# A decode attention kernel on one Trainium2 core: keys moving past stationary queries, softmax along the free axis, exponentials turned in 32x32 squares by VectorE

## The chip, the cores and the metric

The kernel runs on one core of one Trainium2 chip. The metric is the device time of one execution in microseconds. Three runs of the kernel before gave 127.4, 127.41 and 128.99 us, median 127.41 us. One further execution was profiled: it took 127.15 us, of which the profile's span (first to last instruction) is 125.4 us, at a mean granted TensorE clock of 0.97.

## What is computed

One decode step for a batch of B = 8 tokens: a layer norm, grouped-query attention over the last 1024 of 4096 cached keys, and a gated feed-forward part whose result multiplies the attention's. All inputs are bfloat16.

```python
# x: [8, 1, 512]; k_cache, v_cache: [8, 8, 4096, 128]; wq: [512, 4096]; wo: [4096, 512]
# w_gate, w_up: [512, 1792]; w_down: [1792, 512]
xn = layernorm(A_x)
W  = 1024                                             # window: the last W keys
q  = (xn @ wq) as [8, 32 heads, 1, 128]
k  = repeat(k_cache[:, :, 4096 - W:, :], 4, axis=1)   # 8 key heads, each for 4 query heads
v  = repeat(v_cache[:, :, 4096 - W:, :], 4, axis=1)
p  = softmax(einsum("bhqd,bhkd->bhqk", q, k) * 128 ** -0.5)
s  = einsum("bhqk,bhkd->bhqd", p, v) as [8, 1, 4096] @ wo
g  = silu((gelu(xn @ w_gate) * (xn @ w_up)) @ w_down)
out = A_x + s * g
```

The names B_x and A_x are two inputs; the kernel, like the reference, feeds the normalised A_x to both parts.

## The kernel before

Keys and values are read in 16 **quads** (`NQ`). A quad is one key head and four batch rows (`QG` = 4), 1024 keys each: 1 MB of keys and 1 MB of values. `load_set` brings one such megabyte in one DMA, issued by SP, into one of 16 ring buffers `ring_sb` of 128 partitions by 8 KB. Each partition holds 32 consecutive keys of one batch row. The DRAM side of that copy is written `"g (e c) d -> e g (c d)"`: the outer count is e (32 blocks of 32 keys), the next is g (the 4 batch rows), the inner run is 32 keys by 128 values, 8 KB. So the rows of the tile go 4 to a block: partition 4e + g.

SP issues all loads of the kernel in one fixed order: the feed-forward weights (w_gate, w_up, w_down), wq, the first two key quads (`LAG` = 2), then for every quad the keys of the quad two ahead and its own values, and after every second quad half a megabyte of wo. A tile of the ring is taken again once the work on its old content has ended. At most some eight loads are on their way at a time.

The order of the compute is written out by hand. After the feed-forward part and the query projection (with dummy matmuls, `keep_busy`, between them) the main loop runs over q = 0 to 17 and, in each, over four **steps** i. A step does on TensorE: eight transposes of 128x128 key squares into PSUM (`transposes`), eight score matmuls (`scores`) in which the transposed keys are stationary and 16 query columns move, and eight value matmuls for the quad two before (`values`). The transposed keys go from PSUM to SBUF in two parts, 640 columns by VectorE (`kTa`) and 384 by ScalarE (`kTb`).

Scores come out with keys on partitions and, in the free axis, 32 key columns by 16 query columns (4 batch rows by 4 heads), so three quarters of what is computed is between the key of one batch row and the query of another. A matmul per quad (`row_of`, `other`, L382) first puts -1e30 into those places. The maximum over keys is taken along the free axis by VectorE (`max_keys`, L404) and across partitions with a TensorE transpose and another reduction (`max_all`, L412, L414). Two small VectorE operations (L419, L422) lay its negative out on a diagonal, and a 512-column matmul (L433) adds it to the scores in PSUM. ScalarE takes the exponentials (L442). They already have keys on partitions, as `values` needs. `sums` adds them over partitions with eight matmuls by ones (L447) and inverts the sums. `normalise` scales the attention output and `project` multiplies it by wo.

Of the kernel before, what the change touches and what calls it, by code (L numbers as in the profile page):

```python
# [8 lines left out]
ACT = mybir.ActivationFunctionType  # L9
ALU = mybir.AluOpType  # L10
AX = mybir.AxisListType
BF16 = mybir.dt.bfloat16
FP32 = mybir.dt.float32
PSUM = bass.MemoryType.PSUM
# [3 lines left out]
def kernel(  # L18
# [28 lines left out]

    nc = tc.nc
    ctx.enter_context(tc.manual_schedule())

    B, Sq, D = A_x.shape
    Hkv, Sk, Dh = A_k_cache.shape[1], A_k_cache.shape[2], A_k_cache.shape[3]
    Hq = A_wq.shape[1] // Dh
    rep = Hq // Hkv
    W = min(4096, max(256, Sk // 4))
# [10 lines left out]
    QG = 4  # L66
    NB = QG
    NCS = QG * NSC
    VC = 4
    AC = 3  # L70
# [4 lines left out]
    QC = QG * rep  # L75
    SH = B // QG
# [8 lines left out]
    p_pool = ctx.enter_context(tc.tile_pool(name="p_pool", bufs=4))  # L85
# [4 lines left out]
    ps_mx = ctx.enter_context(tc.tile_pool(name="ps_mx", bufs=1, space=PSUM))  # L90
    ps_sum = ctx.enter_context(tc.tile_pool(name="ps_sum", bufs=1, space=PSUM))
# [5 lines left out]
    qT_all = persist.tile([P, B, Hq], BF16, name="qT_all")  # L97
# [12 lines left out]
    def load_set(cache, q):  # L110
        hkv, b = divmod(q * QG, B)
        t = buffer(NL)
        nc.sync.dma_start(
            out=t,
            in_=cache[b : b + QG, hkv, win0:Sk, :].rearrange(
                "g (e c) d -> e g (c d)", c=NCS
            ),
        )
        return t
# [48 lines left out]
    for q in range(NQ):  # L168
# [23 lines left out]
    nc.vector.memset(ones_pp, 1.0)  # L192

    row_of = consts.tile([QG, P // QG, QG], BF16, name="row_of")
    nc.vector.memset(row_of, 0.0)
    nc.gpsimd.affine_select(
        out=row_of,
        in_=row_of,
# [3 lines left out]
        pattern=[[0, P // QG], [1, QG]],  # L202
        channel_multiplier=-1,
    )
    other = consts.tile([QG, QG, rep], BF16, name="other")
    nc.vector.memset(other, MASK)
    nc.gpsimd.affine_select(
        out=other,
        in_=other,
        compare_op=ALU.not_equal,  # L210
        fill=0.0,
        base=0,
        pattern=[[1, QG], [0, rep]],
        channel_multiplier=-1,
    )

    LO = 32
    diag = []
    for i in range(2):
        t = consts.tile([LO + QC, QC], BF16, name=f"diag{i}")  # L220
        nc.vector.memset(t, 0.0)
        diag.append(t)
# [131 lines left out]
    nc.vector.tensor_copy(out=qT_all, in_=qT_ps.rearrange("p h b -> p b h"))  # L354


    kT, sc, pT, mxs, shift, recip = {}, {}, {}, {}, {}, {}

    def transposes(g):
        q, i = divmod(g, NB)  # L360
        kT_ps = ps_kT.tile([P, W], BF16, name="kT_ps")
        for c in range(NSC):
            n = i * NSC + c
            nc.tensor.transpose(  # L364
                kT_ps[:, c * P : (c + 1) * P],
                k_sb[q][:, n * Dh : (n + 1) * Dh],
                ident,
            )
        own = (NSC - AC) * P
        ta = kT_pool.tile([P, own], BF16, name="kTa")  # L370
        nc.vector.tensor_copy(out=ta, in_=kT_ps[:, 0:own])  # L371
        tb = kT_pool.tile([P, W - own], BF16, name="kTb")
        nc.scalar.copy(out=tb, in_=kT_ps[:, own:])  # L373
        kT[g] = [ta[:, c * P : (c + 1) * P] for c in range(NSC - AC)]
        kT[g] += [tb[:, c * P : (c + 1) * P] for c in range(AC)]

    def scores(g):
        q, i = divmod(g, NB)
        hkv, b = divmod(q * QG, B)
        if i == 0:  # L380
            sc[q] = ps_sc.tile([P, NCS, QC], FP32, name="sc_ps")
            nc.tensor.matmul(  # L382
                sc[q],
                row_of.rearrange("g e s -> g (e s)"),
                other.rearrange("g s j -> g (s j)")
                .unsqueeze(1)
                .to_broadcast([QG, NCS, QC]),
                start=True,
                stop=False,
                skip_group_check=True,  # L390
            )
        for c in range(NSC):
            nc.tensor.matmul(  # L393
                sc[q][:, i * NSC + c, :],
                kT[g][c],
                qT_all[:, b : b + QG, hkv * rep : (hkv + 1) * rep],
                start=False,
                stop=False,
                skip_group_check=True,
            )  # L400

    def max_keys(q):
        mx = small.tile([P, QC], FP32, name="mx")
        nc.vector.tensor_reduce(  # L404
            out=mx, in_=sc[q].rearrange("p c n -> p n c"), axis=AX.X, op=ALU.max
        )
        mxs[q] = mx

    def max_all(q):

        mxT_ps = ps_mx.tile([QC, P], FP32, name="mxT_ps")
        nc.tensor.transpose(mxT_ps, mxs[q], ident_f)  # L412
        nm = small.tile([QC, 1], FP32, name="nm")
        nc.vector.tensor_reduce(  # L414
            out=nm, in_=mxT_ps, axis=AX.X, op=ALU.max, negate=True
        )
        eye = ident_f[0:QC, 0:QC]
        parts = diag[q % 2]
        nc.vector.tensor_scalar(  # L419
            out=parts[0:QC, :], in0=eye, scalar1=nm[:, 0:1], scalar2=None, op0=ALU.mult  # L420
        )
        nc.vector.scalar_tensor_tensor(  # L422
            out=parts[LO : LO + QC, :],
            in0=eye,
            scalar=nm[:, 0:1],
            in1=parts[0:QC, :],
            op0=ALU.mult,
            op1=ALU.subtract,
        )
        shift[q] = parts  # L430

    def exponentials(q):
        nc.tensor.matmul(  # L433
            sc[q],
            ones_pp[0 : LO + QC, :],
            shift[q].unsqueeze(1).to_broadcast([LO + QC, NCS, QC]),
            start=False,
            stop=True,
            skip_group_check=True,
        )  # L440
        pT[q] = p_pool.tile([P, NCS, QC], BF16, name="pT")
        nc.scalar.activation(out=pT[q], in_=sc[q], func=ACT.Exp, scale=inv_sqrt_dh)  # L442

    def sums(q):
        sums_ps = ps_sum.tile([P, NB, QC], FP32, name="sums_ps")
        for c in range(NSC):
            nc.tensor.matmul(  # L447
                sums_ps,
                ones_pp,
                pT[q][:, c * NB : (c + 1) * NB, :],  # L450
                start=(c == 0),
                stop=(c == NSC - 1),
            )
        recip[q] = small.tile([P, QC], FP32, name="recip")
        nc.vector.tensor_reduce(  # L455
            out=recip[q],
            in_=sums_ps.rearrange("p c n -> p n c"),
            axis=AX.X,
            op=ALU.add,
        )  # L460
        nc.vector.reciprocal(out=recip[q], in_=recip[q])

    o_ps = {}

    def values(g):
        q, i = divmod(g, NB)
        if i == 0:
            o_ps[q] = ps_o.tile([P, VC, QC], FP32, name="o_ps")
        for c in range(NSC):
            n = i * NSC + c  # L470
            wide = VC if n + VC <= NCS else 1
            nc.tensor.matmul(  # L472
                o_ps[q][:, 0:wide, :],
                v_sb[q][:, n * Dh : (n + 1) * Dh],
                pT[q][:, n : n + wide, :],
                start=(n == 0),
                stop=(n == NCS - 1),
                skip_group_check=True,
            )

    def normalise(q):
        hkv, b = divmod(q * QG, B)
        nc.vector.tensor_tensor(  # L483
            out=oT_all[:, hkv * rep : (hkv + 1) * rep, b : b + QG].rearrange(
                "p j g -> p g j"
            ),
            in0=o_ps[q][:, 0, :].rearrange("p (g j) -> p g j", g=QG),
            in1=recip[q].rearrange("p (g j) -> p g j", g=QG),
            op=ALU.mult,
        )  # L490
# [18 lines left out]
    for q in range(NQ + LAG):  # L509
        v = q - LAG  # L510
        for i in range(NB):
            g = q * NB + i
            if g + 1 < NG:
                transposes(g + 1)
            if i == 1 and 1 <= q <= NQ:
                max_all(q - 1)
            if g < NG:
                scores(g)
            if v >= 0:
                if i == 0:  # L520
                    sums(v)
                values(v * NB + i)
            if i == 2 and 1 <= q <= NQ:
                exponentials(q - 1)
            if v >= SH and v % SH == 0 and i >= NB // 2:
                for h in range(2):
                    project((v // SH - 1) * rep + (i - NB // 2) * 2 + h)
        if v >= 0:
            normalise(v)
        if q < NQ:  # L530
            max_keys(q)
# [6 lines left out]
    sg_ps = ps_mx.tile([B, D], BF16, name="sg_ps", tag="mxT_ps")  # L538
# [35 lines left out]
```

## Time and profile before

| what | value |
|---|---|
| median of three runs | 127.41 us |
| the profiled execution, its own time | 127.15 us |
| its span | 125.4 us |
| TensorE matmul busy | 109.9 us (88%) |
| TensorE weight load busy | 85.5 us (68%) |
| VectorE busy | 64.3 us (51%) |
| ScalarE busy | 42.3 us (34%) |
| read from HBM over the span | 47.46 MB |

The table is read so: a busy TensorE is not TensorE at its peak, since matmuls are pipelined and their modelled durations overlap (a lone 128x128 transpose shows 0.22 us, eight in a row show 0.61 us from first start to last end). Busy shares are averages over the whole span; what limits a stage is seen in that stage's waits.

### The profile page before, as it was taken

The page shows a single profiled execution, that of the slowest core. Times are in us where ns is not written, and L with a number is a line of the kernel's source. Part 1 is how long each engine was busy: PE and PEld are TensorE (multiplying, and loading weights), DVE is VectorE, ACT ScalarE, POOL GpSimd, SP SyncE. Part 2 cuts the span into 40 slices and gives each one's busy share as a digit, 9 for nine tenths or more (in the row PEclk, how much of TensorE's full clock was granted, in tenths as well). Part 3 has the DMA queues.
Part 4 walks back from the last instruction along what each step waited for, and adds up shares of the span by engine and source line. Part 5 has one row for each costly group of instructions (what it writes and reads, how often), then busy time and mean ns, then how long its engine had stood idle before and what let it go on. Part 6 is the DMA issues. An engine that isn't in the chain of part 4 may idle for free.

```text
span 125.4 us, 4892 instructions
## 1 busy us (share of the span) xinstructions
PE 109.9 (88%) x2202; PEld 85.5 (68%) x2202; DVE 64.3 (51%) x200; ACT 42.3 (34%) x86; POOL 1.2 (1%) x7
## 2 busy tenths in 40 slices
PE   5997819897999999999997997969999998999780
PEld 1444315574777888878886876849888886788570
DVE  5200300101467767856866664744676675766531
ACT  4000500000356355453453434342536435344210
POOL 3000000000000000000000000000000000000000
PEclk9999995999999999999999999985999999999999
DMA  3999999999999999999999999999999999999600
GB/s 78 407 418 389 350 405 421 423 421 418 421 415 423 396 421 421 408 415 428 413 404 422 431 406 415 418 431 402 420 422 423 398 425 418 414 398 420 244 32 3
DMA packets 12373, 47.78 MB, mean 381 GB/s; under 512 B 816, under 2 KB 6720, under 8 KB 7744
## 3 DMA queue, kind: packets, MB, share of 16 engines
q1 hardware_dynamic: 12336, 47.46, 93.9%
q8 instruction: 17, 0.28, 0.9%
q14 instruction: 4, 0.03, 0.1%
q10 hardware_dynamic: 16, 0.01, 0.0%
HBM read 47.46 MB, written 0.01 MB: 378 GB/s over the span
## 4 chain that ended last, share of the span: by engine, by line
DMA 44%; PE 32%; SPq 9%; DVE 7%; ACT 4%; issue 2%; ACTq 0%
DMA ring_sb<-in_A_k_cache_dram 30%; DMA ring_sb<-in_A_v_cache_dram 14%; PE kT_ps L364 12%; PE o_ps L472 6%; PE sc_ps L393 6%; SPq L129 4%; DVE kTa L371 4%; ACT kTb L373 4%; SPq L143 3%; PE sc_ps L433 2%; PE sc_ps L382 2%; PE sT_ps L498 2%; PE sums_ps L447 2%; SPq L136 2%; DVE mx L404 1%
## 5 line engine op out<-in xcount | busy, mean ns | idle before, releaser
L373 ACT COPY kTb<-kT_ps 128x384 bf16<-128x384 bf16 x64 | 30.6, 479 | 55.7 <-DVE kTa L371 55.6
L371 DVE COPY kTa<-kT_ps 128x640 bf16<-128x640 bf16 x64 | 31.2, 489 | 23.3 <-PE kT_ps L364 22.7
L364 PE MATMUL kT_ps<-ident,ring_sb 128*128 128x128 bf16 x512 | 39.7, 221 | 3.0 <-DMA ring_sb<-in_A_k_cache_dram 3.0
L364 PEld LDWEIGHTS <-ring_sb 128*128 128x128 bf16 x512 | 29.7, 98 | 5.7 <-DMA ring_sb<-in_A_k_cache_dram 4.6
L472 PE MATMUL o_ps<-pT,ring_sb 128*128 128x64 bf16 (+1 forms) x512 | 24.7, 191 | 0.9 <-issue 0.7
L472 PEld LDWEIGHTS <-ring_sb 128*128 128x128 bf16 x512 | 19.1, 98 | 1.5 <-issue 0.8
L231 PE MATMUL idle_ps<-ones_w 128*128 128x512 bf16 x58 | 17.4, 434 | 1.5 <-DVE ones_w L177 1.5
L393 PEld LDWEIGHTS <-kTa 128*128 128x128 bf16 x320 | 14.8, 97 | 4.4 <-issue 2.0
L393 PE MATMUL sc_ps<-qT_all,kTa 128*128 128x16 bf16 x320 | 17.7, 171 | 0.0
L393 PE MATMUL sc_ps<-qT_all,kTb 128*128 128x16 bf16 x192 | 14.5, 171 | 1.3 <-ACT kTb L373 0.4
L393 PEld LDWEIGHTS <-kTb 128*128 128x128 bf16 x192 | 9.3, 96 | 2.9 <-ACT kTb L373 1.0
L404 DVE TENSOR_REDUCE mx<-sc_ps 128x16 f32<-128x512 f32 x16 | 10.9, 680 | 0.0
L442 ACT ACTIVATE pT<-sc_ps 128x512 bf16<-128x512 f32 x16 | 9.6, 602 | 2.4 <-PE sc_ps L433 2.4
L231 PEld LDWEIGHTS <-ones_w 128*128 128x128 bf16 x58 | 5.0, 102 | 6.3 <-issue 1.7
L433 PE MATMUL sc_ps<-diag,ones_pp 48*128 48x512 bf16 x16 | 6.2, 386 | 0.4 <-DVE diag L422 0.4
L447 PE MATMUL sums_ps<-pT,ones_pp 128*128 128x64 bf16 x128 | 6.5, 195 | 0.0
L382 PE MATMUL sc_ps<-other,row_of 4*128 4x512 bf16 x16 | 6.4, 398 | 0.0
L309 PEld LDWEIGHTS <-ring_sb 128*128 128x128 bf16 x56 | 2.3, 107 | 5.4 <-DMA ring_sb<-in_B_w_down_dram 3.8
L498 PEld LDWEIGHTS <-wo_sb 128*128 128x128 bf16 x128 | 4.3, 96 | 2.4 <-issue 2.4
L455 DVE TENSOR_REDUCE recip<-sums_ps 128x16 f32<-128x64 f32 x16 | 3.6, 224 | 4.3 <-PE sums_ps L447 4.3
L498 PE MATMUL sT_ps<-oT_all,wo_sb 128*128 128x8 bf16 x128 | 5.4, 167 | 0.3 <-DVE oT_all L483 0.3
L309 PE MATMUL fT_ps<-hT_sb,ring_sb 128*128 128x8 bf16 x56 | 2.3, 170 | 3.3 <-DMA ring_sb<-in_B_w_down_dram 3.3
(54 smaller groups left out, 58.7 us busy)
## 6 DMA issues: line engine op xcount, KB each, us to landing
ring_sb<-in_A_k_cache_dram SPq DMA_DIRECT2D x16, 1024.0 KB, 18.7
ring_sb<-in_A_v_cache_dram SPq DMA_DIRECT2D x16, 1024.0 KB, 18.6
ring_sb<-in_A_wq_dram SPq DMA_DIRECT2D x4, 1024.0 KB, 14.3
wo_sb<-in_A_wo_dram SPq DMA_DIRECT2D x8, 512.0 KB, 17.5
ring_sb<-in_B_w_gate_dram SPq DMA_DIRECT2D x2, 896.0 KB, 4.7
ring_sb<-in_B_w_up_dram SPq DMA_DIRECT2D x2, 896.0 KB, 8.1
ring_sb<-in_B_w_down_dram SPq DMA_DIRECT2D x2, 896.0 KB, 14.1
x_sb<-in_A_x_dram ACTq DMA_DIRECT2D x1, 8.0 KB
```

What stands on the lines that cost most here:

```text
L231: nc.tensor.matmul(idle_ps, ones_w[:, 0:P], ones_w, start=True, stop=True)
L364: nc.tensor.transpose(kT_ps[:, c * P : (c + 1) * P], k_sb[q][:, n * Dh : (n + 1) * Dh], ident,)
L371: nc.vector.tensor_copy(out=ta, in_=kT_ps[:, 0:own])
L373: nc.scalar.copy(out=tb, in_=kT_ps[:, own:])
L382: nc.tensor.matmul(sc[q], row_of.rearrange("g e s -> g (e s)"), other.rearrange("g s j -> g (s j)") .unsqueeze(1) .to_broadcast([QG, NCS, ...
L393: nc.tensor.matmul(sc[q][:, i * NSC + c, :], kT[g][c], qT_all[:, b : b + QG, hkv * rep : (hkv + 1) * rep], start=False, stop=False, skip_g ...
L404: nc.vector.tensor_reduce(out=mx, in_=sc[q].rearrange("p c n -> p n c"), axis=AX.X, op=ALU.max)
L433: nc.tensor.matmul(sc[q], ones_pp[0 : LO + QC, :], shift[q].unsqueeze(1).to_broadcast([LO + QC, NCS, QC]), start=False, stop=True, skip_gr ...
L442: nc.scalar.activation(out=pT[q], in_=sc[q], func=ACT.Exp, scale=inv_sqrt_dh)
L447: nc.tensor.matmul(sums_ps, ones_pp, pT[q][:, c * NB : (c + 1) * NB, :], start=(c == 0), stop=(c == NSC - 1),)
L472: nc.tensor.matmul(o_ps[q][:, 0:wide, :], v_sb[q][:, n * Dh : (n + 1) * Dh], pT[q][:, n : n + wide, :], start=(n == 0), stop=(n == NCS - 1 ...
L498: nc.tensor.matmul(sT_ps[0][:, d, :], wo_sb[:, h, d * P : (d + 1) * P], oT_all[:, h, :], start=(h == 0 and d == 0), stop=(h == Hq - 1), sk ...
```

## The change

Five things change together.

The **layout of the loads**: the DRAM side of `load_set` is written `g e (c d)` in place of `e g (c d)`. The bytes, the 128 rows of 8 KB and the ring buffers are the same; partition 32g + e now holds block e of batch row g, so a batch row fills one quadrant of 32 partitions.

The **scores**: the queries are stationary and the transposed keys move. `qT_all` holds, for each quad and each batch row, 32 columns of which four are queries and the rest are zeros. Four matmuls per step, one per quadrant of the output, each with 32 stationary columns and 256 moving columns, taken from the transposed keys in eight runs of 32. The mask matmul is gone.

The **softmax**: a partition now holds one query of one batch row (16 of the 128 partitions do; the rest hold zeros). One reduction along the free axis gives the maximum (`maxima`), one small operation the bias (which is -1e30 on the unused partitions), and the exponential takes the bias and also returns the sum of each row. The cross-partition maximum, the diagonals and the two 512-column matmuls are gone. The sum is inverted, spread over 16 columns, and one float32 matmul by ones per quad brings the inverses to all partitions, in place of eight matmuls.

The **exponentials are transposed** back to keys on partitions by one VectorE instruction per quad, which turns 32x32 squares. `values` then moves 2 x 32 columns in place of 4 x 16.

The **evacuation of the transposed keys** is no longer shared: VectorE copies all 1024 columns in even steps, ScalarE in odd steps. Within a step, `values` now comes ahead of `scores`.

```diff
@@ layout of the loads (load_set)
             in_=cache[b : b + QG, hkv, win0:Sk, :].rearrange(
-                "g (e c) d -> e g (c d)", c=NCS
+                "g (e c) d -> g e (c d)", c=NCS
             ),
@@ constants: row_of, other and diag go
+    ones_f = consts.tile([P, P], FP32, name="ones_f")
+    nc.vector.memset(ones_f, 1.0)
+    nc.vector.memset(qT_all, 0.0)
+    own = consts.tile([P, QG, rep], FP32, name="own")
+    nc.vector.memset(own, 0.0)
+    nc.gpsimd.affine_select(out=own, in_=own, compare_op=ALU.not_equal, fill=1.0,
...
+    off = consts.tile([P, 1], FP32, name="off")
+    nc.vector.tensor_reduce(out=off, in_=own, axis=AX.XY, op=ALU.max)
+    nc.vector.tensor_scalar(out=off, in0=off, scalar1=-MASK, scalar2=MASK, ...
@@ queries
-    nc.vector.tensor_copy(out=qT_all, in_=qT_ps.rearrange("p h b -> p b h"))
+    for g in range(QG):
+        nc.vector.tensor_copy(
+            out=qT_all[:, :, g, g * rep : (g + 1) * rep].rearrange(
...
@@ transposes
-        nc.vector.tensor_copy(out=ta, in_=kT_ps[:, 0:own])
-        nc.scalar.copy(out=tb, in_=kT_ps[:, own:])
+        kT[g] = kT_pool.tile([P, W], BF16, name="kT")
+        if i % 2 == 0:
+            nc.vector.tensor_copy(out=kT[g], in_=kT_ps)
+        else:
+            nc.scalar.copy(out=kT[g], in_=kT_ps)
@@ scores: the mask matmul and eight matmuls per step go
+        for n in range(QG):
             nc.tensor.matmul(
+                sc[q][n * QP : (n + 1) * QP, i * BK : (i + 1) * BK],
+                qT_all[:, q, n, :],
+                kT[g].rearrange("p (c g e) -> p g c e", c=NSC, g=QG)[:, n],
                 start=True,
+                stop=True,
+            )
@@ max_keys and max_all go
+    def maxima(q):
+        mx = small.tile([P, 1], FP32, name="mx")
+        nc.vector.tensor_reduce(out=mx, in_=sc[q], axis=AX.X, op=ALU.max)
+        bias[q] = small.tile([P, 1], FP32, name="bias")
         nc.vector.tensor_scalar(
+            out=bias[q], in0=mx, scalar1=-inv_sqrt_dh, scalar2=off[:, 0:1], ...
@@ exponentials: the 512-column matmul goes
+        nc.scalar.activation(out=p, in_=sc[q], func=ACT.Exp, scale=inv_sqrt_dh,
+            bias=bias[q], accum_out=total)
+        pT[q] = pT_pool.tile([P, NCS, QP], BF16, name="pT")
+        nc.vector.transpose(pT[q].rearrange("p c j -> p (c j)"), p)
+        nc.vector.tensor_scalar(out=total, in0=total, scalar1=0.5, ..., op0=ALU.max)
+        nc.vector.reciprocal(out=total, in_=total)
+        nc.vector.tensor_scalar(out=own_recip[q], in0=own..., scalar1=total[:, 0:1], ...
@@ sums: eight matmuls and a reduction go
+        nc.tensor.matmul(
+            sc[q][:, 0:QC], ones_f, own_recip[q], start=True, stop=True
+        )
+        nc.vector.tensor_copy(out=recip[q], in_=sc[q][:, 0:QC])
@@ main loop
+            if i == 0 and 1 <= q <= NQ:
+                maxima(q - 1)
             if g + 1 < NG:
                 transposes(g + 1)
-            if i == 1 and 1 <= q <= NQ:
-                max_all(q - 1)
+            if v >= 0:
+                values(v * NB + i)
             if g < NG:
                 scores(g)
-            if v >= 0:
-                if i == 0:
-                    sums(v)
-                values(v * NB + i)
-            if i == 2 and 1 <= q <= NQ:
+            if i == 1 and 1 <= q <= NQ:
                 exponentials(q - 1)
...
+            if i == NB - 1 and 1 <= q <= NQ:
+                sums(q - 1)
```

## The prediction, made before the changed kernel was run

> **What bounds the kernel now.** I read first the span in slices, then the table of DMA queues, then the chain of waits, and last the DMA issues and stretches of the timeline.
>
> ```profile
> DMA  3999999999999999999999999999999999999600
> GB/s 78 407 418 389 350 405 421 423 421 418 421 415 423 396 421 421 408 415 428 413 404 422 431 406 415 418 431 402 420 422 423 398 425 418 414 398 420 244 32 3
> ...
> DMA packets 12373, 47.78 MB, mean 381 GB/s; under 512 B 816, under 2 KB 6720, under 8 KB 7744
> ...
> q1 hardware_dynamic: 12336, 47.46, 93.9%
> ...
> q10 hardware_dynamic: 16, 0.01, 0.0%
> ...
> DMA 44%; PE 32%; SPq 9%; DVE 7%; ACT 4%; issue 2%; ACTq 0%
> ```
>
> The 16 DMA engines are full from about 2.5 us to 118 us. 47.46 MB at the 416 GB/s of the stretch from 60 to 90 us take 114 us of a span of 125.4. TensorE, 88% busy, runs just beside that: one quad needs 2.10 MB of keys and values and on average 0.26 MB of wo, 2.36 / 0.416 = 5.67 us, and the chain shows 4.9 to 5.4 us of TensorE work per quad. So the transfers set the pace, compute fits under them, and only the last 7 us lie behind the data.
>
> The issues say how deep that queue is:
>
> ```profile
> ring_sb<-in_A_k_cache_dram SPq DMA_DIRECT2D x16, 1024.0 KB, 18.7
> ring_sb<-in_A_v_cache_dram SPq DMA_DIRECT2D x16, 1024.0 KB, 18.6
> ...
> x_sb<-in_A_x_dram ACTq DMA_DIRECT2D x1, 8.0 KB
> ```
>
> A megabyte takes 18.7 us to land because about 7.8 MB (18.7 x 0.416) are on their way together. SP waits for earlier loads, not for compute alone.
>
> **How a copy is dealt out to the engines.** This is the part of the change that I weigh most, and the packet counts carry it. Count the data packets on q1: 32 key and value loads of 128 rows (4096), 4 gate and up loads of 128 x 2 (1024), 2 down loads of 128 x 7 (1792), 4 wq loads of 128 (512), 8 wo loads of 128 x 4 (4096), and the output's 8 rows: 11528. The page has 12336, so 808 more. Those are 50 loads x 16, and 8 for the output. On q10 the 8-row load of x shows 16 packets, 8 rows and 8 more. The small packets agree: 50 x 16 + 8 + 8 = 816, the page's count under 512 B to the packet. So every engine that a copy runs on closes it with one small packet: loads of 128 rows run on 16 engines, copies of 8 rows on 8. Two rules fit all 52 copies. Either the engines follow the outermost count of the access (128, or 32 for the keys' DRAM side, gives 16; 8 gives 8), or they follow the number of rows.
>
> The changed load writes its DRAM side with g outermost: 4, then 32. By the first rule each megabyte goes to 4 engines, by the second still to 16. For the first speaks that issuing costs SP as little for 896 packets (476 ns at the least, w_down) as for 128 (535 ns at the least, keys): whatever deals the packets out is not walking rows, so it can cut only at a count that the instruction carries. Against it speaks only that no copy here has an outermost count of 4.
>
> [...]
>
> **The sum, with four engines.** Keys and values are 32 x 1.0486 = 33.55 MB, 8.39 MB for each of four engines. The other 13.91 MB stay on 16, 0.87 MB each. So the four carry 9.26 MB each, in place of 2.97. Rate of one engine: 416 / 16 = 26.0 GB/s in the stretch named, 432 / 16 = 27.0 in the best stretch (18 to 20 us), 402 / 16 = 25.1 in one of the poorer slices. I take 26.5, between the first two, since with twelve engines quiet whatever they share is idle: 9.26 / 26.5 = 349.4 us. Transfers run from 2.5 us, so they end at 351.9.
>
> [...]
>
> Behind the last byte comes what comes now behind the last values: from the 32 value matmuls at 119.95 us to the end, 5.45 us. TensorE will have stood still by then:
>
> ```profile
> 16.00:18.00 2.00, 0.33 (x7) 0.24 (x7) 0.00 (x0) 0.00 (x0) 0.00 (x0) 1.00 1.10 405
> 18.00:20.00 2.00, 1.31 (x24) 0.87 (x25) 0.00 (x0) 0.00 (x0) 0.00 (x0) 0.76 1.04 432
> 20.00:22.00 2.00, 2.00 (x23) 0.91 (x21) 0.00 (x0) 0.00 (x0) 0.00 (x0) 0.50 0.99 414
> ```
>
> (The columns are the stretch, its length, busy time of TensorE, weight load, VectorE, ScalarE and GpSimd, the granted clock, DMA share and GB/s.) After 2 us with little work the clock falls to 0.50, so the 2.0 us of TensorE in that tail (1.07 + 0.54 + 0.39) double: 7.45 us. The last 32.8 KB of wo on each engine, 1.24 us, come after the last values and lie beside their matmuls: minus 1.24. Span 351.9 + 6.2 = 358.1. The profiled execution has 127.15 - 125.4 = 1.75 us around its span: 359.9, and as the median of the runs is 0.26 us from that execution, 360 us stands for both.
>
> **The rest of the change hides under 20 us per quad** (2.10 MB on four engines). I price it for the case that it must fit under 5.67.
>
> TensorE per quad. Gone: the mask matmul (0.32 us of the chain), the maximum's transpose (0.11), the diagonal matmul (0.32), eight sum matmuls (0.25), 32 score matmuls (4 x 0.18 to 0.29). Added: 16 score matmuls of 256 columns. The dummy matmuls of 512 columns follow each other at 0.20 us (five in 1.24 with 0.43 for the last), so 0.10 each, 1.6 in all; less, down to 0.4, if the four quadrants run side by side, up to 3.2 if the 64-byte runs of the moving keys are read at half rate; I take 1.6, that row's value. One float32 matmul of 16 columns: 0.03 to 0.28 (the float32 transpose); 0.1. The value matmuls move 64 columns as before. Together -1.9 + 1.7: nothing, with a loss of up to 1.6 us per quad if the reads are slow.
>
> VectorE per quad. Gone: four 640-column copies (1.96), the two reductions over maxima (0.68 + 0.27), 0.22 x 2, the sums' 0.22. Added: two 1024-column copies, each 0.49 to 0.78 (the 640-column row, and that scaled by columns), I take 0.75; a reduction of the same 512 elements, 0.68; the squares, bounded by 0.49 (the 512-column memset) and 0.68 (that reduction), 0.65; five small ones of about 0.22. Sum 3.9 against 3.6 gone: +0.3, with 4.1 used before of 5.67.
>
> ScalarE per quad. Gone 4 x 0.48. Added two 1024-column copies: 0.48 for 384 and 0.60 for 512 elements make 0.96 ns per element, so 1.09 us each (0.48 to 1.28 as bounds), and 0 to 0.3 for returning the sums. 2.9 against 2.5.
>
> At the start VectorE clears qT_all (512 elements took 0.48 us; four times that at worst, 1.9) and its reduction of `own` waits for GpSimd; layer norm statistics stand behind it, and TensorE's first products behind those, 1 to 2 us later. Keys land after 31 us, the loads ahead do not wait for compute: no cost. The four query copies (0.4 to 1.7 us in all against 0.43) come before the first keys land.
>
> **The rivals.**
>
> *Rows decide: 16 engines, the transfers still set the pace.* For it: the second rule fits the counts as well. Transfers end near 118 us as before. The new tail misses the diagonal steps and the cross-partition maximum of the last quad (about 1.5 us from 117.5 to 119), and gains a square transpose: 1 to 2 us less, none if TensorE is behind at the end anyway. 124 to 128 us, say 126. It ends on the other side: not slower.
>
> *16 engines, but the scores become the bound.* If the moving keys are read at half rate, a quad takes 4.9 + 1.6 = 6.5 us against 5.67; 0.83 x 16 = 13 us more, about 140. From 0.8 us of added TensorE work per quad on, it decides. No row shows a moving operand in such runs.
>
> **How the numbers follow.** Four engines 0.84: the outermost rule fits all 52 copies and is the only one that goes with the issue times; rows 0.11; slow scores 0.04; the rest 0.01. Rates of 27.0 and 25.1 give 353 and 379. As no bulk copy here ran on few engines, I allow 5% more rate than the best stretch (28.4 GB/s: 336) and 1.5% more time than the poorest: 336 to 385. This holds nine tenths of the 0.84, near 8 in 10 in all, and reaching to the rivals would add only empty space. Faster or slower by 2% is what a measurement can tell here. Of the rows' 0.11 I give 0.05 to faster and 0.06 to same, the rest's 0.01 to same: slower 0.88.
>
> **What would show it.** Right: the packets of a key load closed by 4 in place of 16, so 50 x 16 + 16 = 816 small packets become 18 x 16 + 32 x 4 + 16 = 432; about 106 GB/s over most of the span; landing times near 8 x 10 us; a chain almost all DMA; TensorE busy under a third, clock near 0.5 to 0.7. Wrong: 816 again, and 410 GB/s. If 432 holds and the time lies outside the range, the rate of an engine by itself was what I misjudged.

## The result, and the profile after

The changed kernel takes 380.22 us at the median of four runs (374.87 to 387.39) against 127.41 before. The runs of 374.87 and 377.7 us are in the faster of two states and give the ratio, 2.946 times the kernel before (95% interval 2.901 to 2.991), while the profiled execution, 382.73 us, is in the slower. The forecast was 360 us with a range of 336 to 385. The profile's span is 380.9 us, at a mean granted TensorE clock of 0.572.

The page of the changed kernel, its span in 40 slices of 9.5 us, packets, main queue and chain of waits:

```profile
PE   7892543242234343243334343143334342142523
...
PEclk9967566565555555565655555555655555555655
DMA  8982224222233222422242222422224222423320
GB/s 310 380 350 70 98 107 136 105 106 102 97 123 112 107 101 107 135 106 102 105 139 103 102 102 105 136 108 102 103 106 136 104 103 106 137 106 127 106 96 26
DMA packets 11986, 47.73 MB, mean 125 GB/s; under 512 B 432, under 2 KB 6336, under 8 KB 7360
...
q1 hardware_dynamic: 11952, 47.46, 33.1%
...
DMA 82%; SPq 10%; PE 6%; issue 0%; DVE 0%
```

For the first 27 us, while the weights load, the rows look as before. Then the digit of DMA falls to 2 and the rate from 380 GB/s in the second slice to between 97 and 107 in the slices that hold loads of keys and values alone: about a quarter of the 416 before. Small packets are 432, the number that 32 copies closed by 4 packets each give, beside 18 closed by 16 and the 16 of the two small copies. The chain is 82% DMA, and TensorE, waiting most of the time (40% busy), is granted about half its clock (0.572).

Below, TensorE's pieces that a landing released, in order of time (start, length, instructions, and in brackets the idle time before and its cause):

```profile
83.64 1.04 PE L364 MATMUL kT_ps<-ident,ring_sb 128*128 128x128 bf16 x8 [5.53 <-DMA ring_sb<-in_A_k_cache_dram]
93.58 0.61 PE L443 MATMUL o_ps<-pT,ring_sb 128*128 128x64 bf16 x8 [6.77 <-DMA ring_sb<-in_A_v_cache_dram]
105.77 1.03 PE L364 MATMUL kT_ps<-ident,ring_sb 128*128 128x128 bf16 x8 [7.79 <-DMA ring_sb<-in_A_k_cache_dram]
117.56 0.61 PE L443 MATMUL o_ps<-pT,ring_sb 128*128 128x64 bf16 x8 [8.63 <-DMA ring_sb<-in_A_v_cache_dram]
127.41 1.03 PE L364 MATMUL kT_ps<-ident,ring_sb 128*128 128x128 bf16 x8 [5.14 <-DMA ring_sb<-in_A_k_cache_dram]
...
374.42 1.86 PE L443 MATMUL o_ps<-pT,ring_sb 128*128 128x64 bf16 x32 [7.21 <-DMA ring_sb<-in_A_v_cache_dram]
```

Every megabyte is waited for. Landings that nothing disturbs are 9.9 us apart (83.64 to 93.58, 117.56 to 127.41), others 11 to 12. The last values land at 374.4 us, and 6.5 us later the span ends.

### The profile page after: what moved, and what is told of

It is laid out like the page before. It is cut to its first block, busy times and chain, and to the rows that moved or that the text cites. A ratio compares the mean times of both kernels' runs of the same rounds, so it can differ in the third digit from the quotient of the medians.

```text
span 380.9 us, 4056 instructions
## 1 busy us (share of the span) xinstructions
PE 151.5 (40%) x1797; PEld 114.2 (30%) x1802; DVE 80.2 (21%) x188; ACT 53.9 (14%) x70; POOL 0.7 (0%) x6
## 4 chain that ended last, share of the span: by engine, by line
DMA 82%; SPq 10%; PE 6%; issue 0%; DVE 0%
DMA ring_sb<-in_A_k_cache_dram 60%; DMA ring_sb<-in_A_v_cache_dram 19%; SPq L116 10%; DMA ring_sb<-in_B_w_down_dram 3%; PE kT_ps L364 3%; PE o_ps L443 1%; PE sc_ps L380 1%; PE sc_ps L430 1%; SPq L139 1%; PE sT_ps L469 0%; PE sg_ps L509 0%; DVE out_sb L511 0%; DVE oT_all L454 0%; DVE sg L506 0%
## 5 line engine op out<-in xcount | busy, mean ns | idle before, releaser
L364 PE MATMUL kT_ps<-ident,ring_sb 128*128 128x128 bf16 x512 | 65.7, 310 | 105.5 <-DMA ring_sb<-in_A_k_cache_dram 105.5
L364 PEld LDWEIGHTS <-ring_sb 128*128 128x128 bf16 x512 | 52.0, 146 | 116.4 <-DMA ring_sb<-in_A_k_cache_dram 109.1
L443 PE MATMUL o_ps<-pT,ring_sb 128*128 128x64 bf16 (+1 forms) x512 | 38.5, 242 | 115.4 <-DMA ring_sb<-in_A_v_cache_dram 115.4
L371 DVE COPY kT<-kT_ps 128x1024 bf16<-128x1024 bf16 x32 | 22.1, 692 | 245.7 <-PE kT_ps L364 245.7
L373 ACT COPY kT<-kT_ps 128x1024 bf16<-128x1024 bf16 x32 | 32.4, 1013 | 286.6 <-PE kT_ps L364 286.6
L443 PEld LDWEIGHTS <-ring_sb 128*128 128x128 bf16 x512 | 33.8, 133 | 119.5 <-DMA ring_sb<-in_A_v_cache_dram 119.3
L380 PE MATMUL sc_ps<-kT,qT_all 128*32 128x256 bf16 x256 | 25.5, 390 | 0.0
L413 DVE STREAM_TRANSPOSE pT<-p 128x1024 bf16<-128x1024 bf16 x16 | 19.8, 1236 | 1.4 <-ACT p L404 1.4
L390 DVE TENSOR_REDUCE mx<-sc_ps 128x1 f32<-128x1024 f32 x16 | 19.5, 1216 | 0.0
L404 ACT ACTIVATE p<-sc_ps,bias 128x1024 bf16<-128x1024 f32 x16 | 17.9, 1120 | 2.6 <-DVE bias L392 2.6
L430 PE MATMUL sc_ps<-own_recip,ones_f 128*128 128x16 f32 x32 | 9.4, 373 | 0.0
L339 PEld LDWEIGHTS <-ring_sb 128*128 128x128 bf16 x128 | 4.0, 101 | 1.7 <-issue 1.2
L264 PEld LDWEIGHTS <-ring_sb 128*128 128x128 bf16 x112 | 3.7, 104 | 1.6 <-issue 1.3
```

Of the source, the lines that this page charges most:

```text
L364: nc.tensor.transpose(kT_ps[:, c * P : (c + 1) * P], k_sb[q][:, n * Dh : (n + 1) * Dh], ident,)
L371: nc.vector.tensor_copy(out=kT[g], in_=kT_ps)
L373: nc.scalar.copy(out=kT[g], in_=kT_ps)
L380: nc.tensor.matmul(sc[q][n * QP : (n + 1) * QP, i * BK : (i + 1) * BK], qT_all[:, q, n, :], kT[g].rearrange("p (c g e) -> p g c e", c=NSC, ...
L390: nc.vector.tensor_reduce(out=mx, in_=sc[q], axis=AX.X, op=ALU.max)
L404: nc.scalar.activation(out=p, in_=sc[q], func=ACT.Exp, scale=inv_sqrt_dh, bias=bias[q], accum_out=total,)
```

## The experiments

Two questions are asked. Is it the outermost count alone that makes the kernel slow? And can the new layout be loaded at full rate?

### The layout alone, and the outermost count as a dose

**before_g_major**: one part of the change alone, in the kernel before.

```diff
-                "g (e c) d -> e g (c d)", c=NCS
+                "g (e c) d -> g e (c d)", c=NCS
...
-        pattern=[[0, P // QG], [1, QG]],
+        pattern=[[1, QG], [0, P // QG]],
```

> The kernel before with the layout of the loads alone changed to g outermost (and the pattern of its mask constant, so that it still masks the right rows); all compute as before. Theory: four engines, 432 packets under 512 B, about 106 GB/s, 365 to 385 us. Rival two (the new softmax is the cost): 127 us.

Measured: 383.28 us, one run. Its packets:

```profile
DMA packets 11989, 47.78 MB, mean 125 GB/s; under 512 B 432, under 2 KB 6336, under 8 KB 7360
```

One string in the loads, with the mask constant that follows it and the old softmax in place, gives the loss. The new compute is not needed for it; a share of a few microseconds could not be told here, as the changed kernel's own four runs lie 12.5 us apart.

**outer_eight** and **outer_two**: other outermost counts, at the same bytes and the same number of loads.

```diff
-            in_=cache[b : b + QG, hkv, win0:Sk, :].rearrange(
+            in_=cache[:, hkv, lo : lo + W // SH, :].rearrange(          # outer_eight
+            in_=cache[b : b + QG // 2, hkv, Sk - 2 * W : Sk, :].rearrange(   # outer_two
```

> The changed kernel with sets of 512 keys of all eight batch rows in place of 1024 keys of four, so that the outermost count is 8; same bytes, same number of loads. The compute still treats a set as 1024 keys of four rows, so what is computed differs and only the time is read. Theory: eight engines, 18 x 16 + 32 x 8 + 16 = 560 packets under 512 B, about 212 GB/s, 33.55 / 8 + 0.87 = 5.06 MB per engine at 26.5 GB/s = 191 us, 195 to 215 in all. Rival one (streams 8.4 MB apart are slow in themselves): no better than 300 us.

> The changed kernel with sets of 2048 keys of two batch rows in place of 1024 keys of four, so that the outermost count is 2 (partitions 0 to 63 hold one batch row, 64 to 127 the other); same bytes, same number of loads. The compute still treats a set as 1024 keys of four rows, so what is computed differs and only the time is read. Theory (outermost count): two engines, 18 x 16 + 32 x 2 + 16 = 368 packets under 512 B, 53 GB/s, 33.55 / 2 + 0.87 = 17.65 MB per engine at 26.5 GB/s = 666 us, 670 to 700 in all. It also asks about the start: with four engines the first load of keys moved at only 61 to 82 GB/s for some 12 us and then at 106. If that comes from neighbouring quarters of the partitions being filled in step by engines that share a way into SBUF (lower or upper half), two engines that fill one half each have nothing to share: 53 GB/s from the first load on. If a start is slow for another reason: 30 to 41 GB/s for the first 10 us or more.

Measured: 224.66 us for eight, 687.39 us for two, one run each. The page's packets and the rate over a long stretch (the columns of a stretch are those of the prediction), first of eight:

```profile
DMA packets 12114, 47.73 MB, mean 214 GB/s; under 512 B 560, under 2 KB 6464, under 8 KB 7488
```

```profile
60.00:200.00 140.00, 87.08 (x1126) 69.41 (x1124) 57.17 (x128) 39.23 (x50) 0.00 (x0) 0.64 0.56 210
```

and of two, with its first stretches of key loads:

```profile
DMA packets 11922, 47.73 MB, mean 70 GB/s; under 512 B 368, under 2 KB 6272, under 8 KB 7296
```

```profile
28.00:30.00 2.00, 1.95 (x36) 1.25 (x36) 0.00 (x0) 0.00 (x0) 0.00 (x0) 0.86 0.14 53
30.00:32.00 2.00, 1.97 (x38) 1.38 (x38) 0.13 (x1) 0.00 (x0) 0.00 (x0) 1.00 0.12 49
...
34.00:36.00 2.00, 0.00 (x0) 0.00 (x0) 0.00 (x0) 0.00 (x0) 0.00 (x0) 0.84 0.13 53
36.00:38.00 2.00, 0.00 (x0) 0.00 (x0) 0.00 (x0) 0.00 (x0) 0.00 (x0) 0.50 0.13 53
```

Small packets are 368, 432 and 560 for outermost counts of 2, 4 and 8, each to the packet as worked out, and the undisturbed rates 53, 106 and 210 GB/s: 26.3 to 26.5 GB/s per engine. That settles the number of engines for these counts, and rival one of outer_eight (streams far apart are slow in themselves) falls, since eight streams run at twice the rate of four. The time of two lies in its range, the time of eight 10 us above; it too starts slowly, at 123 to 176 GB/s until about 50 us, which two does not. With 16 (lower_upper, below) and 32 (the kernel before) all engines are busy, a DMA share of 1.02 from 40 to 110 us in both; what other counts below 32 do no run shows.

### Sixteen engines in the new layout: not enough

**split_rows** undoes the count and keeps the layout: one copy per batch row, 32 rows each. **order_0213** and **two_queues** change its order, or issue half of the copies from GpSimd.

```diff
-        nc.sync.dma_start(
-            out=t,
-            in_=cache[b : b + QG, hkv, win0:Sk, :].rearrange(
-                "g (e c) d -> g e (c d)", c=NCS
-            ),
-        )
+        for g in range(QG):            # order_0213, two_queues: for g in (0, 2, 1, 3)
+            nc.sync.dma_start(         # two_queues: g = 2, 3 on nc.gpsimd
+                out=t[g * QP : (g + 1) * QP, :],
+                in_=cache[b + g, hkv, win0:Sk, :].rearrange(
+                    "(e c) d -> e (c d)", c=NCS
+                ),
+            )
```

> The changed kernel with one thing undone: each megabyte of keys or values is brought by four copies, one per batch row, each with 32 as its outermost count on both sides; the layout in SBUF and all compute stay. Theory (the outermost count picks the engines): every copy is closed by 16 small packets, so 18 x 16 + 128 x 16 + 16 = 2352 packets under 512 B; the DMA engines are full again at about 416 GB/s, the data ends near 118 us, and the time is 123 to 130 us. Rival one (reading four batch rows 8.4 MB apart, or filling the partitions in this order, is slow in itself): more than 300 us. Rival two (the new softmax is the cost): at least 140 us with the DMA engines idle part of the time.

Measured: 201.75 us (197.9 to 210.52, four runs). Neither theory nor rival had this. The page:

```profile
DMA  6999999999999999999999999999999999999820
GB/s 213 419 363 403 424 287 223 223 223 225 216 230 225 226 219 216 231 239 236 225 233 236 236 239 247 251 239 237 232 256 241 233 226 249 234 217 218 206 52 2
DMA packets 13906, 47.74 MB, mean 239 GB/s; under 512 B 2352, under 2 KB 8256, under 8 KB 9280
```

2352 small packets: all loads of keys and values run on 16 engines, and the DMA row shows all engines busy to the end. But they move 225 GB/s in most of the first slices and 231 from 40 to 140 us, where the kernel before moves 416. By these rates a packet of 8 KB takes nearly twice as long as before (416 / 231 = 1.8, an estimate); the engines are full and little more than half as fast. So a second limit lies behind the first. The next runs ask whether it is the size of a copy (256 KB, rival S) or the 32 neighbouring partitions that a copy fills (theory P).

**quarter_copies**: the kernel before, with four copies per megabyte cut by columns.

```diff
+        for k in range(4):
+            nc.sync.dma_start(
+                out=t[:, k * n : (k + 1) * n],
+                in_=src[:, :, k * n : (k + 1) * n],      # src: "g (e c) d -> e g (c d)"
+            )
```

> The kernel before with each megabyte brought in four copies of 256 KB, cut by columns, so that every copy still fills all 128 partitions (with rows of 2 KB). In the run with four copies per megabyte, one per batch row, all 16 engines were busy at 225 GB/s in place of 416. Theory P (what halves the rate is that a copy fills 32 neighbouring partitions only): the data still ends near 118 to 122 us, 126 to 132 us in all. Rival S (copies of 256 KB are slow in themselves): about 225 GB/s here too, 195 to 205 us.

> Four copies per megabyte, one per batch row, as in the run before, all issued by SP, but in the order 0, 2, 1, 3 of the batch rows (and so of the quarters of the partitions) in place of 0, 1, 2, 3. Theory P with quarters 0 and 1 sharing their way into SBUF, and 2 and 3 another: engines that run ahead of others by one copy now meet the other half, so some gain, 160 to 195 us. Theory P with every quarter limited by itself: the same either way, 198 to 205. [...] Rival S: 198 to 205.

> Four copies per megabyte again, but batch rows 0 and 1 are issued by SP and 2 and 3 by GpSimd, so that copies into the lower and the upper half of the partitions are on their way together (constants are set up ahead of the loads, as GpSimd makes some of them). Theory P with halves: both halves fill at once, 350 to 416 GB/s, 127 to 150 us. Theory P with every quarter by itself: at most the same. Rival S: 195 to 205 us.

**keys_in_one**: the new compute, the keys in one copy of the old layout, the values in four copies in the order of order_0213.

```diff
+        if cache is A_k_cache:     # keys: one copy, "g (e c) d -> e g (c d)"; values: four, g in (0, 2, 1, 3)
...
-                kT[g].rearrange("p (c g e) -> p g c e", c=NSC, g=QG)[:, n],
+                kT[g].rearrange("p (c e g) -> p g c e", c=NSC, g=QG)[:, n],
```

> The changed kernel with the keys loaded in one copy per megabyte as in the kernel before (outermost count 32, partition 4e + g), the moving keys picked with a stride of four columns in place of runs of 32; only the values keep the new layout, in four copies per megabyte in the order 0, 2, 1, 3, all by SP. Theory P: keys at 416 GB/s, values at 225, so 2.5 + 4.7 us and 0.63 of wo per quad, 16 x 7.8 + 26 + 7 = 158 us, 140 to 165. It also shows whether the new compute, with keys as fast as before, is ever what is waited for. Rival S: 158 as well; but if strided moving keys hold TensorE up, matmuls of the scores get longer than 0.40 us per step at half clock and 170 us or more.

Measured, one run each: 142.99, 179.97, 211.0 and 186.69 us. Stretches of the four, in this order:

```profile
40.00:110.00 70.00, 59.67 (x1210) 50.78 (x1207) 38.86 (x118) 25.67 (x54) 0.00 (x0) 0.90 1.02 351
```

```profile
40.00:140.00 100.00, 73.47 (x997) 59.47 (x995) 53.88 (x114) 37.48 (x48) 0.00 (x0) 0.70 1.02 270
```

```profile
54.00:160.00 106.00, 67.92 (x922) 53.64 (x920) 45.33 (x99) 32.68 (x41) 18.09 (x38) 0.71 1.03 237
```

```profile
60.00:160.00 100.00, 67.00 (x912) 52.69 (x910) 46.89 (x102) 33.93 (x43) 0.00 (x0) 0.69 1.03 250
```

Copies of 256 KB that fill all partitions run at 351 GB/s in 2 KB rows: slower than a whole megabyte (416), but not halved. The 142.99 us lie in neither range, but rival S falls as the main cause. The order of the quarters matters (270 against 231 GB/s over the same 100 us in split_rows), as theory P with halves has it. The two mixed forms missed by much. In two_queues GpSimd's copies ran ahead of SP's by the depth of the ring and crowded the weights (the last part of the query projection began at 58 us in place of 30), and once both queues took turns the rate was 237, not 350: halves issued from two queues did not add up. In keys_in_one the keys did not regain 416 GB/s between copies of values (250 over both). The strided keys are not the reason: its score matmuls stay at 0.40 us per step, the bound named above, and the DMA engines are busy throughout (a share of 1.03). Why is not settled.

**lower_upper** and **column_halves** put the question with less around it: two copies of 512 KB per megabyte in the kernel before, once by partitions, once by columns.

```diff
+        for k in range(2):     # rows = P // 2, n = NL // 2
+            out=t[k * rows : (k + 1) * rows, :], in_=src[k * rows // QG : (k + 1) * rows // QG]   # lower_upper
+            out=t[:, k * n : (k + 1) * n],       in_=src[:, :, k * n : (k + 1) * n]               # column_halves
```

> The kernel before with each megabyte in two copies of 512 KB, the first filling partitions 0 to 63, the second 64 to 127; outermost count 16, rows of 8 KB, so 16 engines. Theory P with halves (64 neighbouring partitions take no more than half the rate): about 225 to 300 GB/s, 165 to 205 us. Theory P with quarters by themselves, or rival S for 256 KB copies: 390 GB/s or more, 127 to 135 us.

> The control for the run before it: the kernel before with each megabyte in two copies of 512 KB cut by columns, so that each fills all 128 partitions with rows of 4 KB. Theory P: 127 to 134 us, whatever the run before it shows. If copies of 512 KB are slow in themselves it is as slow as that one.

Measured: 187.3 and 127.98 us, one run each. The same stretch of both, lower_upper first:

```profile
40.00:110.00 70.00, 52.84 (x836) 44.35 (x833) 29.11 (x84) 19.04 (x39) 0.00 (x0) 0.70 1.02 243
```

```profile
40.00:110.00 70.00, 65.36 (x1451) 55.44 (x1449) 47.03 (x140) 31.42 (x65) 0.00 (x0) 1.00 1.03 408
```

The same number of copies of the same size, on 16 engines, with the engines full in both (a share of 1.02 and 1.03): 243 GB/s when a copy fills 64 neighbouring partitions, 408 when it fills all 128. A copy into one half of the partitions ran at little more than half the rate (0.60 of it), though its outermost count of 16 kept all engines busy. Theory P with quarters by themselves, which asked for 390 GB/s or more here, is out. Where copies of 256 KB go to the quarters in turn the rate is 223 GB/s in the first slices and 231 from 40 to 140 us (split_rows); where each goes to the other half than the one before it, 270 over the same stretch (order_0213). From this difference the author takes it that copies into different halves overlap to a degree; why one half by itself takes little more than half the rate no view shows.

### The start and the loads of wo

In the changed kernel the first loads of keys move slowly. The same view, before any wo is on its way:

```profile
28.00:30.00 2.00, 1.93 (x44) 1.41 (x44) 0.00 (x0) 0.00 (x0) 0.00 (x0) 1.00 0.26 66
...
34.00:36.00 2.00, 0.00 (x0) 0.00 (x0) 0.00 (x0) 0.00 (x0) 0.00 (x0) 0.50 0.25 70
...
40.00:42.00 2.00, 0.00 (x0) 0.00 (x0) 0.00 (x0) 0.00 (x0) 0.00 (x0) 0.50 0.26 98
42.00:44.00 2.00, 1.34 (x13) 1.34 (x14) 0.27 (x1) 0.00 (x0) 0.00 (x0) 0.50 0.26 106
```

Four engines are busy throughout (a DMA share of 0.22 to 0.28), yet at 66 GB/s first and 106 after 14 us. before_g_major (61 GB/s first, 98 after 14 us) and wo_first (61 and 106) show the same. In outer_two, where by the theory two engines fill one half of the partitions each, the rate is 53 GB/s from the first stretch. That is what was expected if engines that fill neighbouring quarters in step hinder each other until they drift apart. It fits. No view shows single engines, but the end of wo_first (the run below) shows that they do come apart: with only the last load under way, the DMA share falls from 0.23 to 0.13 at 361 us and stays there, at 49 to 57 GB/s, until 367, so two of the four engines had finished some 6 us before the others. That it is the neighbouring quarters that hinder each other remains argued.

**wo_first** takes wo out of the stream.

```diff
+    for hkv in range(Hkv):
+        load_wo(hkv)
     for q in range(LAG):
         load_k(q)
...
-        if q % SH == SH - 1:
-            load_wo(q // SH)
```

> The changed kernel with all of wo loaded ahead of the first keys in place of half a megabyte after every second quad. Undisturbed key loads land 9.9 us apart in the profile, 26.5 GB/s per engine, and those beside a load of wo 11 to 12 us apart, some 3.2 us per load of wo where its bytes alone ask for 1.24. Theory A (wo among the keys is what the prediction's sum missed): wo costs 10 us ahead in place of 8 x 3.2 = 26, so 358 to 364 us. Rival (the four engines simply run slower over a long time): 370 to 380 us.

Measured: 372.6 us at the median (369.71 to 376.83, four runs); by the two shortest runs 2.901 times the kernel before, interval 2.883 to 2.919. Theory A promised 358 to 364; about 7 of some 16 us came. The median lies in the rival's range, but the rival's reason does not hold: from 136.68 to 345.07 us of the trace 21 loads in a row land 9.92 us apart. In the whole trace, 31 loads from the first keys (53.26 us) to the last values (368.52) take 315.3 us; at 9.9 us each they would take 306.9. So 8.4 us of disturbance are left with no wo in sight, nearly all in two places (102.98 to 126.76 and 345.07 to 368.52). In the first of them, from 108 to 122 us, four engines are busy (a DMA share of 0.24 to 0.26) and move only 82 to 98 GB/s, as at the start. In the changed kernel the same 31 loads take 374.42 - 42.66 = 331.8, 24.9 too many. So 16.5 us go with wo: its bytes ask for 8.7 of them (seven loads at 1.24), and 7.8 are hold-up beyond the bytes. What makes the other 8.4 stays open; the profiled execution took 376.83 us and the two shortest 369.7 and 369.8, so most of it may belong to that execution alone.

outer_two has the same loads of wo. There, loads that nothing disturbs land 19.84 us apart and those beside wo 20.6 to 21.4, so wo costs 0.8 to 1.5 us, its bytes and no more. In these traces the slow start and the hold-up go together: both are there with four engines, neither with two.

### The rest of the change at full rate

**old_layout** keeps all the new compute and loads as before.

```diff
-                "g (e c) d -> g e (c d)", c=NCS
+                "g (e c) d -> e g (c d)", c=NCS
...
-                kT[g].rearrange("p (c g e) -> p g c e", c=NSC, g=QG)[:, n],
+                kT[g].rearrange("p (c e g) -> p g c e", c=NSC, g=QG)[:, n],
```

> The changed kernel with the loads of keys and values in the layout of the kernel before (one copy per megabyte, outermost count 32); the moving keys are picked with a stride of four columns. The weights then stand on other partitions than their values, so the attention output is weighted wrongly and the run is read for its time alone: it is the rest of the change at full transfer rate. Theory, as the prediction's first rival has it: transfers set the pace, 416 GB/s, data ends near 118 us, 124 to 128 us. Rival V (VectorE, measured now at 4.9 us per quad of 5.67, and the longer chain through maximum, exponential and squares become the bound): 130 to 145 us, with TensorE waiting for VectorE or ScalarE in its place. Rival T (TensorE, moving keys with a stride): score matmuls longer than those of the changed kernel, 135 us or more.

Measured: 131.66 us (131.53 to 131.72, four runs) against 127.16; ratio 1.0347, interval 1.033 to 1.0364. The theory's 124 to 128 us missed, and the time lies in rival V's range, but VectorE does not limit the loop. The loop keeps up: from 40 to 110 us this kernel moves 417 GB/s, the kernel before 416. The loss lies behind the data. The end of its timeline, and below it the same two ends of the tail in the kernel before (the last maximum and the last values):

```profile
117.65 1.22 DVE L390 TENSOR_REDUCE mx<-sc_ps 128x1 f32<-128x1024 f32 x1
...
119.23 1.11 ACT L404 ACTIVATE p<-sc_ps,bias 128x1024 bf16<-128x1024 f32 x1 [2.95 <-PE o_ps L443]
...
120.47 1.25 DVE L413 STREAM_TRANSPOSE pT<-p 128x1024 bf16<-128x1024 bf16 x1 [1.35 <-ACT p L404]
...
122.36 0.58 PE L430 MATMUL sc_ps<-own_recip,ones_f 128*128 128x16 f32 x2 [2.95 <-DVE own_recip L420]
...
123.44 1.84 PE L443 MATMUL o_ps<-pT,ring_sb 128*128 128x64 bf16 x32 [0.49 <-DVE oT_all L454]
```

```profile
116.76 0.68 DVE L404 TENSOR_REDUCE mx<-sc_ps 128x16 f32<-128x512 f32 x1
...
119.95 1.07 PE L472 MATMUL o_ps<-pT,ring_sb 128*128 128x64 bf16 x32
```

Maximum, exponential, squares and three small operations follow each other, and the last values wait for all of it, since the sums stand before them on TensorE: 5.8 us from the maximum of the last quad to its values, against 3.2 before (116.76 to 119.95). TensorE idles meanwhile, and the rest runs at a granted clock of 0.50 (before, 1.00 up to 124 us), 6.5 us in place of 5.45. With the 0.9 us by which the last maximum begins later, as VectorE is still at the quad before, 2.6 + 1.0 + 0.9 = 4.5, the difference of the spans (129.9 and 125.4).

No run here beats the kernel before. The squares need the values in quarters by batch row, and no form of loading them so kept the full rate: 270 GB/s at the most (order_0213), against 416.

## Why the prediction was right, and where it was off

**Four engines**: right, and shown four ways: 432 small packets, the layout alone giving 383 us, and 2 and 8 engines for 2 and 8. The rule of rows, the first rival's ground, is out.

**26.5 GB/s per engine**: right for undisturbed loads, where 9.9 us for 1.0486 MB is 105.9 GB/s.

**9.26 MB at that one rate**: the step that was mis-sized. By the sum, the last values were to land at 351.9 - 1.24 = 350.7 us; in the profile they landed at 374.4. Of the 23.7 us the weights' end takes 1.4 (about 26.8 us, an estimate from the DMA share of 26 to 28 us, for 25.4), the slow start 6 (the first keys took 15.9 us, not 9.9), and disturbances among the other loads 16: 24.9 us beyond 31 x 9.9, where the seven loads of wo ahead of the last values were priced at 1.24 us each, 8.7 in all. The sum took four engines that never hinder each other. It priced wo as if it only added to the stream; wo_first shows that it also held the stream up, for 7.8 of the 16 us. The other 8.4 are not explained. The profiled execution is also a long one: the shortest run took 374.87 us, 7.9 less, and how its loads landed is not on record. So 380 us lies where the prediction's poorest rate, 25.1 GB/s, had put it (379), but by luck: undisturbed engines ran at 26.5 and lost their time in the start and the disturbances.

**The tail**: 6.5 us where 7.45 was said. The clock was 0.50 as foreseen, but only the value matmuls (1.07 to 1.86 us) and the last transposes (0.39 to 0.59) became longer; the 16 matmuls by wo, of 8 columns, went from 0.54 to 0.57 only.

**The rest hides**: right in the changed kernel, where VectorE is 21% busy. Its prices were not:

```profile
L413 DVE STREAM_TRANSPOSE pT<-p 128x1024 bf16<-128x1024 bf16 x16 | 19.8, 1236 | 1.4 <-ACT p L404 1.4
L390 DVE TENSOR_REDUCE mx<-sc_ps 128x1 f32<-128x1024 f32 x16 | 19.5, 1216 | 0.0
L404 ACT ACTIVATE p<-sc_ps,bias 128x1024 bf16<-128x1024 f32 x16 | 17.9, 1120 | 2.6 <-DVE bias L392 2.6
```

The free axis has 1024 elements, since a partition now holds one query with all 1024 keys of its batch row. The prediction took the 512 of the old scores for the reduction (0.68) and the squares (0.65), and left the exponential at its old price. All three are 1.8 to 1.9 times that. VectorE's total rises from 64.3 to 79.4 us in old_layout, 0.94 us per quad and not 0.3. The first rival's 126 us fails with them, as far as old_layout stands for it: at full rate the change costs 4.5 us and does not save 1 to 2. Of these, 2.6 are the longer row of maximum, exponential and squares behind the last scores.

**Scores**: priced at 1.6 us per quad with a bad case of 3.2. The chain of old_layout shows 0.33 us per step, 1.3 per quad, against 0.72 to 1.16 before (four steps of 0.18 to 0.29). The bad case did not come.

**The signs**: 432 packets, about 106 GB/s, the chain of DMA and the clock came as named. Landing times near 80 us did not (36.7, see below), nor a TensorE busy under a third: it shows 40%, as its pieces last longer at half the clock (a transpose 310 ns, 221 before).

## What to carry to other kernels

Before changing the nesting of a load's address pattern, count the small packets that close a copy in the profile: here they told on how many engines it ran, and an outermost count of 4 left twelve of sixteen idle (432 small packets, 106 GB/s in place of 416). Then ask which partitions a copy fills, for a copy into 64 neighbouring partitions ran at 243 GB/s where one of the same size into all 128 ran at 408. By these runs a layout that helps the compute should be one that a single copy can load over all partitions with an outermost count such as the 32 that ran at 416 GB/s; and when new shapes replace old ones, take the elements per partition from the new tile and not from the row it replaces.

## What the runs showed that was not expected

Loads on four engines held SP up. In the kernel before, a copy lands 18.7 us after its issue with some 7.8 MB under way; here a key load landed 36.7 us after its issue (132.75 to 169.51 in the chain), 3.7 loads of 9.9 us, and SP spent most of its time inside load instructions of about 10 us each, their waits included:

```profile
48.33 9.57 SPq L116 DMA_DIRECT2D ring_sb<-in_A_v_cache_dram  x1
57.95 0.47 SPq L154 DMA_DIRECT2D wo_sb<-in_A_wo_dram  x1
58.54 21.97 SPq L116 DMA_DIRECT2D ring_sb<-in_A_k_cache_dram  x1
80.61 9.82 SPq L116 DMA_DIRECT2D ring_sb<-in_A_v_cache_dram  x1
```

So fewer bytes were under way on four engines than on sixteen, some 3.9 MB (an estimate, 3.7 x 1.0486) against 7.8. What limits their number no view shows.

The pattern of the moving keys shows in the score matmuls. Four of a step, from first start to last end as the profile models it, take 0.40 us in the changed layout at half clock (eight transposes beside them 1.03 us) but 0.29 at full clock (transposes 0.62): so in 29 of 32 such steps of two_queues and 24 of 26 of order_0213. There the keys move in runs of 32. In old_layout and keys_in_one, which pick every fourth column, a step takes 0.39 to 0.40 us at the full clock too. So the stride costs 0.11 us per step, 0.44 per quad: rival T of old_layout was right in that, though not in its 135 us.
